# Block-sparse attention with a gated FFN: first loads split by head, row-tiled matmuls in all units, a new written order

## The chip, the cores and the metric

The kernel runs on one core of a Trainium2 chip. The metric is device time in microseconds (us) of one execution; lower is better. Three timed runs of the kernel before gave a median of 282.53 us (282.47 to 284.15).

## What is computed

```python
B, H, S, D = 4, 8, 768, 64
scores = q @ k.T / 8                       # per batch and head
mask   = window of +-1 block | first and last block row and column
         | 3 sampled blocks per block row  # blocks of 32
attn   = softmax(where(mask, scores, -1e9))
x      = (attn @ v), heads side by side    # 3072 tokens x 512
out    = (sigmoid(x @ w_gate) * (x @ w_val)) @ w_out   # 512 -> 1536 -> 512
```

Inputs and output are float32; the kernel computes in float16 with float32 sums.

## The kernel before, in words

**Units.** The work is cut into 12 units of 256 query tokens: 4 batches of 3 units. A unit has 4 pairs of heads. A pair has 3 steps (`Step`): each makes the scores of 256 keys by 256 queries for both heads (`qk`, line 546), ScalarE takes the exponential of the 128x1024 tile into a ring buffer `P` (`exp`, line 569), and VectorE multiplies it by the 0/1 mask (`mul`, line 574). In unit 0 the mask is added before the exponential instead, by extra matmuls of `bias` and the block-spread matrix `e64`, so its steps have twice the matmuls and no multiplication. After the three steps `pv` (line 595) multiplies P by `v` with a column of ones beside it (65 columns), `norm` divides by the sum on VectorE, and the pair's rows are turned into `xT`. Units 0 and 1 turn them by matmul (`turn`, line 623) with a copy out of PSUM (`evac`, on VectorE or ScalarE); later units use a DMA transpose (`xbar`, line 666).

**FFN.** Once all four pairs of a group of units are in `xT`, `Ffn.f` (line 735) makes the gate and value products, ScalarE takes tanh, VectorE multiplies them into `ht`, and `y` makes the output rows, which are copied out and stored. The first four groups are one unit each (matmuls of 256 columns), the last four are two units each (512 columns).

**Two ways to run a product of 128 rows.** `turns` (line 340) cuts each product into two of 64 rows, which run side by side in the two row halves of TensorE's array, on two PSUM banks; for that a job is run in two parts, and between them TensorE waits for the first part's last matmul (`nop`, line 345), so other work is put between. `whole` (line 357) issues one matmul over all 128 rows, in one part. Units below `WIDE = 2` use `whole` for PV and for the FFN's first products (`value`, line 634, and line 775); all the others use `turns`. Scores always have 64 rows. The last unit's output (`y_last`, line 889) is whole in both versions. The transposes of keys and queries that were loaded as 16 bit run in quarters of the array (64*64).

**Order.** Nothing reorders the instructions: a planner made the string `ORDER` (line 39) beforehand, which lists all tasks by number in the order in which every engine issues them, with the PSUM bank (`:2`, four banks m0 to m3), the engine where there are two (`A` ScalarE, `D` VectorE), and gates for loads (`@`). `j3` is a pair of matmuls of zeros (`idle`, line 313) into bank 3.

**Start.** SyncE's queue issues the constants, then the first two heads' keys as float32 (`k32`, lines 246 to 254); ScalarE's queue issues the sampled blocks, those heads' queries (`q32`), and one copy of the spread matrix; GpSimd's queue issues the other copy of it (line 256), for which it waits until VectorE has cleared `e64`, and then all that is in `FIRST` (line 36): keys, queries and values of the other heads, then the FFN's weights. The float32 heads are cast and paired (`pair`, line 473), turned by matmul (`turn`, line 477) and copied to `kT` and `qT`. `mask_blocks` (line 290) makes the block mask from the constants and the sampled blocks, and matmuls of it with `e64` (line 397) spread it to `bias` and `mb24`.

Of the kernel before, what the change touches and what calls it, by code (L numbers as in the profile page):

```python
# [12 lines left out]
f16 = mybir.dt.float16  # L13
# [22 lines left out]
FIRST = "k1 q1 v0 k2 q2 v1 k3 q3 v2 v3 r0 w0 r1 w1 r2 w2 r3 w3 w4 w5 o0 o1 o2"  # L36
FFN_LAG = 3
VW = 96
ORDER = """
j3 j3 j3 j3 0 j3 j3 j3 11D 1:0 8A 3:1 5D 12:2 6:3 4A 7D 2 13A 80:3 106:1 9:0 30:2 107A 10D 81D  # L40
15:1 31 34:0 16D j3 76:3 17:2 35 32:1 18D 77D 74:2 33 40:0 14 20:3 75D 41 44:1 21D 22:2 45 19 36:0
23D 25:3 27:2 37 26D 215@30 50:1 28D 46:3 51 82:2 48:0 83D 47 64:1 49 84:2 60:0 85D 65 38:3 29 61
56:2 39 66:1 57 42:0 67D 54:3 43D 52:1 165:0 53D 55 93:2 24 58:1 166 94 99:3 59 68:2 95:0 100 96D
181:1 69D 62:0 182 63D 78:3 102:2 162:0 79D 144@102 103 70:1 126:3 125@50 71D 183 163 164 111:1
127 119:2 131:0 120 128 167 112 104 138:3 122:2 132 145:1 123 133 121 139 124 169:0 146 140 147
72:2 170 86:3 159:1 73D 87 171 152:2 160 205:0 153 108:3 88 89:1 206 105@89 90 101 174:2 92@165
154 109 187@89 207 239:1 91 235@86 175 155:0 188:3 110 156 114@40 176 168@155 240 113 115:0 157
189 141:2 116 202:1 142 190 195:0 203 143 196 232:3 172:2 233 129:0 173 97:3 191:2 130 204 192A
193 98A 117:0 256 212:2 194 216 118A 213 184:3 177:0 217 178A 185 134:2 148:0 218 149D 135D 241
242:0 198:3 221A 252:2 214 199 136 179 219A 258 180 246:3 200 253 227 137 254 268:1 247 257 243  # L50
248 150 229:2 234 151 269 209:3 300:0 210 270 259 161 230 237 197 293:1 296:3 228 301 284:2 231
297 302 238 244 294 280:0 186 287:3 285 201@280 211 281 286 249:1 298 288 277:0 223:2 289 278 250
224 251 336:3 327:0 337 158@336 225 274 264:1 279 261:2 271:3 265 295 236 328 262 266 272 310:1
329 273 311 226 263 307:2 320:3 255 340 308 290 312 303:1 321 309 323:2 341 282 324 333:3 208 304
378@333 322 342 334 305 347:2 345A 343D 351:3 314:1 245@351 352 348 338 372:0 315 299@64 349 373
365:3 316 357@181 369 375:2 353 386:0 403@239 358:1 376 317 374 366 387 377 325 354:2 359 367 355
368 404:0 360 356 432:3 400:2 405 433 361 313@400 260 393:1 326@307 401 335 411:3 267@333 406 402
418:2 394 419 424@418 412 407 283@138 395 362:0 413 389:2 379:1 390 414 363 397:3 425:2 364 398
388 383 466:0 380 420 467 330 370 435:3 426 391 381 436 382 439:0 346 415 399 427 408:1 421:3 428
440 220 422 275 222 470:2 291 409 344 471 331 473:3 441 434 332 474 318 476:2 410 276 475 487:3  # L60
446:1 477 488 416 319 472 452 447 423 417 449:3 437 453 478 384 450 463:1 479 292 454 464 489
442:3 385 448 493:2 457A 451 455A 443 371 516:1 465 494 517 444 507:0 429 430 495 518 459:3 490:1
496 508 491 468 483:2 509 492 504:1 510 460 505 484 461 480:0 506 469 485 542:1 497:3 543 486 481
456 498 482 519:2 431 511:1 520 499 501:0 576:3 462 521 512 502 536:2 500 503 513 522:0 577 514
537 515 526:1 538 558:3 523 544 559 527 524 555:2 549:3 528 556 306 539 608:1 525 550 609 560 552
532:2 644:0 551 533 529:1 645 534 597:2 562 530 646 563 557 598 594:0 564 578 392@594 595 531
601:1 633@421 565D 567A 561@32 627:2 569:0 610 628 573:3 579@141 570 602 438@122 571 574 629
339@555 630:2 587:0 631 596 704@50 647:3 575 588 548@397 603 648 604 600@470 580:2 396 683@209 589
662:1 545:3 581 668@165 663 590 632 619:0 546 622:1 664 582 599 620 611:3 623 583 612 621 615:2
624 665:3 625 673:0 666 616 547 350 674 756:1 614@40 634:3 675 757 710 695 584:0 553 617 635 445  # L70
718@435 618 651:1 636 535@662 585 650@102 680:2 652 586 681 637 684:0 653 613 677:2 701:3 654 685
678 606 642 638:1 607 702 696 669:2 686 639 591 712:3 670 640 713 687 458 655:1 605 671 682 715:3
691:0 592 716 659 649 656 540 758 554 705:3 657 714 692 658 568 641 672 753:1 706 693 754 694 566
719:2 593 717 707 698:0 746:1 720 708 643 747 660 721 703 699 661 729:3 726:1 732 730 700 667
739:0 727 733 679 731 743:3 740 744 734 741 755 688:1 752 735A 722:0 728 689 737A 723 690 787:3
749:2 788 724 801:1 572 742 798:0 745 790:3 750 799 748 709 751 791 766:0 541 802 792 769:3 759
770 711 772:1 767 760 773 768 676 844:3 779:0 761 775:1 762A 764D 845 780 763 818:2 776 781 800
804:3 777 774 819 793:0 778 805 771 820 857:1 794 858 782:2 795 835:1 806 796 807 815:0 783 816
789 829:3 836 784 830 785 821:0 859 837 808:2 803 822 838 811:3 823 817 860:1 809 824 861 812 810
832:0 831 828 825:1 813 863:2 833 814 697 826 864 827 786 834 847:3 854:0 848 839:1 626 862 843  # L80
865 855 875:3 840 856 876 738 846 797 870:0 841 850:3 842 765 874 849 878:1 871 879 866 736 851
872 867:2 873 852 881:1 853 898:0 868 877 899 925:3 882 869 926 892:0 883 944:2 886:3 893 945 884
725 895:1 887 880 889:2 894 890 896 928:3 904 891 929 888 962:2 905 963 897 911:3 914 915:1 973:2
906 916 885 912 909A 921:1 913 974 946 922 924 927 923 907D 970:3 941:2 900 931 971 901:0 942 972
918:3 932 917 919 933 902 947:2 934D 954:3 936A 975 903 959:0 965:1 960 943 948 961 955 949 966
950 956 938:0 957 967 983:2 968 939 1004:3 976:1 940 1005 990:0 984 991 987:3 977 985 988 986
993:0 978 1016:2 980:3 1017 979 994 930 1011:1 995 981 996 1050:2 1012 982 1051 920 1007:0 1013
1052 1001:3 951:2 1014 1002 1008 992 952 1061:1 1022:3 953 1062 964 969 1042:2 1009 1003 1019:1
958 989 1023 1020 1010 1043 1024 1021 1053:1 1025 1044 1058:0 1045 997:3 1059 1054 998 1060 1055
1029:2 1035:0 999 1030 1056 1015 1026:3 1036 1018 1063 1027 1037 1047:2 1082:1 1006 1048 1031 1083  # L90
1028 1039:2 1038 1046 1071:3 1040 1032:0 1084 1041 908 1033 1049 1000 1072 1064:2 1034 1057 1073
1067:0 1065 1081 1068 1085 1069 937 1066 1070 1086 935 1074 910 1075 1087 1076 1090D 1100:3 1091
1079D 1096:0 1077D 1078 1101 1080 1097 1102 1132:2 1103 1098 1088A 1108:3 1099 1089 1120:1 1109
1112:0 1110 1121 1111 1113 1122 1092:3 1123 1114 1124:1 1115 1133 1093 1104:0 1094 1125 1095 1105
1126 1134 1136:3 1127 1106 1135 1116:1 1107 1128:2 1117 1137 1118 1129 1119 1138 1140:0 1139 1130
1141 1131 1142 1150:1 1151 1152 1143 1153 1144 1154 1145 1160:3 1146A 1148D 1161 1147 1162 1149
1155:2 1163 1156 1164 1157 1158 1159
"""
GAP, PV_HALF, F_HALF, Y_ONE = 0.3, 0.36, 0.875, 0.216
WIDE = 2  # L100
# [20 lines left out]
class Plan:  # L121
# [4 lines left out]

    def __init__(self, order, idle, hold):
        self.order, self.idle, self.hold = order.split(), idle, hold
        self.tasks, self.last = [], {}
# [5 lines left out]
    def run(self):  # L135
        done = set()
        for token in self.order:
            if token[0] == "j":
                self.idle(int(token[1:]))
                continue  # L140
            i, eng, slot, gate = re.fullmatch(r"(\d+)([PADGS]?)(?::(\d))?(?:@(\d+))?", token).groups()
            i = int(i)
            engines, fn, deps, more = self.tasks[i]
            assert i not in done and done.issuperset(deps)
            done.add(i)
            if slot is not None:
                more["take"].slot = int(slot)
            self.last[i] = fn(eng or engines[0][0])
            if gate is not None:
                self.hold(self.last[i], self.last[int(gate)])  # L150
# [4 lines left out]
def kernel(  # L155
# [46 lines left out]
    e64 = sing.tile([128, S], f16)  # L202
    nc.vector.memset(e64, 0.0)
# [42 lines left out]
    def first_heads(eng, dst, src, t0, t1):  # L246
        eng.dma_start(
            dst[:, :, t0:t1, :],
            src[0, 0:2].rearrange("h (p t) d -> p h t d", t=NT)[:, :, t0:t1, :],
        )  # L250

    nc.sync.dma_start(const, const_h.ap())
    nc.scalar.dma_start(sbi, sampled_blocks)
    first_heads(nc.sync, k32, k, 0, NT)
    first_heads(nc.scalar, q32, q, 0, 2)
    nc.gpsimd.dma_start(e64[0:NB], spread_h.ap())
# [28 lines left out]
    junk = sing.tile([128, 512], f16)  # L285
    nc.vector.memset(junk, 0.0)
# [3 lines left out]
    def mask_blocks(eng):  # L290
        sbf = sing.tile([NB, 3], f32, name="sbf")
# [811 lines left out]
```

## Time and profile before

| | |
|---|---|
| timed runs | 282.47, 282.53, 284.15 us |
| profiled execution | 281.96 us, of which the traced span is 280.2 us |
| mean granted TensorE clock | 0.994 |
| TensorE busy (PE) | 272.4 us, 97% of the span |
| ScalarE busy (ACT) | 192.1 us, 69% |
| VectorE busy (DVE) | 187.9 us, 67% |
| exponentials | 144 of 1.025 us |
| the last matmul ends | 276.97 us into the span |

PE's busy share counts overlapping, pipelined matmuls, so it is read beside the pitch: the time from one start to the next. Times in rows are microseconds from the start of the span; a bracket gives how long the engine was idle before the row and what released it. `64*128` in a matmul's row means that it used 64 rows of the array, `128*128` all of them, `64*64` a quarter.

### The profile page before, as it was taken

The numbers are of one execution on the slowest core, as the hardware profiler recorded it, in microseconds if no ns is written. First come the engines' busy times: TensorE is split into PE (matmuls) and PEld (weight loads), VectorE is DVE, ScalarE is ACT, GpSimd is POOL, SyncE is SP. The second block draws the span as 40 slices with busy tenths as digits, with TensorE's granted clock in tenths as the row PEclk, the third lists the DMA queues.
The fourth block names the chain that finished last, engine by engine and source line by source line (L and its number), as shares of the span: only waits on it lengthen the run. The fifth ranks groups of instructions, "written<-read, shape, count | busy, mean of one in ns | idle before, by whom it ended". The sixth has DMA issues, their size and how long they took to land.

```text
span 280.2 us, 10875 instructions
## 1 busy us (share of the span) xinstructions
PE 272.4 (97%) x4889; PEld 186.1 (66%) x4889; DVE 187.9 (67%) x387; ACT 192.1 (69%) x239; POOL 47.4 (17%) x70
## 2 busy tenths in 40 slices
PE   5999999999999999999999999999999999999995
PEld 2677786777899799766555655666656667555543
DVE  4667894788887888688778746875664888142421
ACT  3798888699897878898668866578677683023301
POOL 8975441011531000082400000000000000000000
PEclk9799999999999999999999999999999999999999
DMA  7999999765589975279967330041100012440003
GB/s 148 184 195 196 200 205 202 110 127 87 77 110 150 206 129 126 40 106 188 125 115 162 68 97 2 12 133 50 30 2 0 6 21 65 117 180 2 0 5 147
DMA packets 56679, 28.92 MB, mean 103 GB/s; under 512 B 33044, under 2 KB 53676, under 8 KB 56632
## 3 DMA queue, kind: packets, MB, share of 16 engines
q0 software_dynamic: 21552, 13.93, 35.6%
q1 hardware_dynamic: 34592, 13.99, 22.7%
q8 instruction: 38, 0.62, 0.9%
q10 hardware_dynamic: 488, 0.30, 0.4%
q14 instruction: 9, 0.07, 0.1%
HBM read 28.47 MB, written 6.29 MB: 124 GB/s over the span
## 4 chain that ended last, share of the span: by engine, by line
PE 91%; DMA 3%; ACT 2%; DVE 2%; issue 1%; SPq 0%; DVEq 0%
PE m L338 89%; DMA xT<-x 2%; DMA e<-bb_spread 1%; ACT P L570 1%; PE m L456 1%; DVE ysb L833 1%; ACT ysb L831 0%; PE m L451 0%; DVE kT L282 0%; DVE mask L282 0%; ACT mask L280 0%; SPq L667 0%; PE m L397 0%; DVE x L616 0%; PE m L315 0%
## 5 line engine op out<-in xcount | busy, mean ns | idle before, releaser
L570 ACT ACTIVATE P<-m 128x1024 f16<-128x1024 f32 x144 | 142.5, 1025 | 31.3 <-PE m L338 27.3
L338 PE MATMUL m<-xT,wv 64*128 64x512 f16 (+2 forms) x672 | 136.1, 331 | 0.3 <-issue 0.3
L338 PE MATMUL m<-xT,wg 64*128 64x512 f16 (+2 forms) x672 | 135.9, 331 | 0.1
L576 DVE TENSOR_TENSOR P<-P,mask 128x1024 f16<-128x1024 f16 x132 | 86.7, 686 | 11.1 <-ACT P L570 10.8
L338 PEld LDWEIGHTS <-wg 64*128 64x128 f16 (+1 forms) x672 | 61.8, 94 | 20.5 <-issue 2.0
L338 PEld LDWEIGHTS <-wv 64*128 64x128 f16 (+1 forms) x672 | 61.8, 94 | 15.9 <-issue 0.3
L338 PE MATMUL m<-wo,ht 64*128 64x512 f16 (+2 forms) x564 | 70.7, 372 | 0.0
L765 DVE SCALAR_TENSOR_TENSOR ht<-th,m 128x512 f16<-128x512 f32 x72 | 49.0, 686 | 30.6 <-ACT th L762 29.6
L762 ACT ACTIVATE th<-m 128x512 f32<-128x512 f32 x72 | 42.7, 598 | 36.0 <-PE m L338 35.3
L338 PE MATMUL m<-qT,kT 64*128 64x256 f16 x576 | 54.0, 272 | 0.3 <-DVE ysb L833 0.2
L338 PEld LDWEIGHTS <-P 64*128 64x128 f16 (+1 forms) x2112 | 46.2, 94 | 9.0 <-issue 1.1
L338 PE MATMUL m<-vex,P 64*128 64x65 f16 (+1 forms) x2112 | 48.2, 190 | 0.0
L338 PEld LDWEIGHTS <-ht 64*128 64x128 f16 (+1 forms) x564 | 30.5, 94 | 21.6 <-issue 1.3
L338 PEld LDWEIGHTS <-kT 64*128 64x128 f16 x576 | 27.4, 95 | 13.0 <-issue 1.7
L220 POOL DMA_DIRECT2D v<-in_v_dram x16 | 11.4, 717 | 65.3 <-PE m L338 56.5
L616 DVE TENSOR_TENSOR x<-m,rz 128x256 f16<-128x256 f32 x48 | 20.4, 425 | 1.7
L615 DVE RECIPROCAL rz<-m 128x4 f32<-128x4 f32 x48 | 8.7, 180 | 17.9 <-PE m L338 16.4
L220 POOL DMA_DIRECT2D q<-in_q_dram x19 | 13.6, 723 | 12.1 <-PE m L338 11.1
L831 ACT ACTIVATE ysb<-m 128x512 f32<-128x512 f32 x13 | 7.5, 597 | 10.6 <-PE m L338 9.9
L833 DVE TENSOR_SCALAR ysb<-m 128x512 f32<-128x512 f32 x9 | 6.1, 688 | 11.8 <-ACT ysb L831 5.5
L220 POOL DMA_DIRECT2D k<-in_k_dram x15 | 10.8, 723 | 6.1 <-PE m L338 5.5
L338 PE MATMUL m<-bias,e 64*128 64x256 f16 x48 | 6.9, 301 | 0.3
(46 smaller groups left out, 69.7 us busy)
## 6 DMA issues: line engine op xcount, KB each, us to landing
out_dram<-ysb SPq DMA_DIRECT2D x23, 256.0 KB, 2.4
v<-in_v_dram POOLq DMA_DIRECT2D x16, 192.0 KB, 5.5
k<-in_k_dram POOLq DMA_DIRECT2D x15, 192.0 KB, 5.9
q<-in_q_dram POOLq DMA_DIRECT2D x12, 192.0 KB, 7.1
wg<-in_moe_w_gate_dram POOLq DMA_DIRECT2D x6, 256.0 KB, 8.6
wv<-in_moe_w_val_dram POOLq DMA_DIRECT2D x6, 256.0 KB, 8.9
wo<-in_moe_w_out_dram POOLq DMA_DIRECT2D x3, 512.0 KB, 12.8
xT<-x SPq DMA_TRANSPOSE x40, 3.2
```

Source lines behind the costliest of these rows:

```text
L220: return nc.gpsimd.dma_start(dst[:, h0:h1, t0:t1, :], src[b, h0:h1].rearrange("h (p t) d -> p h t d", t=NT)[:, :, t0:t1, :],)
L338: return nc.tensor.matmul(out, lhsT, rhs, start=start, stop=stop, skip_group_check=True).ins
L456: nc.tensor.transpose(out16[a * D : (a + 1) * D, h, i * D : (i + 1) * D], tile_[rows, a], ident[rows, rows],)
L570: nc.scalar.activation(self.pt.rearrange("a h i n -> a (h i n)"), both(self.bank).rearrange("a h n -> a (h n)"), AF.Exp, bias=0.0, scale=SCALE
L576: nc.vector.tensor_tensor(self.pt, self.pt, m.unsqueeze(1).broadcast_to([128, 2, 2, UQ]), op=ALU.mult,)
L615: nc.vector.reciprocal(rz, self.acc[:, :, :, D : D + 1])
L616: nc.vector.tensor_tensor(self.x16.rearrange("a s h d -> a h s d"), self.acc[:, :, :, 0:D], rz.broadcast_to([128, 2, 2, D]), op=ALU.mult,)
L762: nc.scalar.activation(th, both(bank)[:, 0, :], AF.Tanh, bias=0.0, scale=0.5)
L765: nc.vector.scalar_tensor_tensor(self.ht[:, tiles[0] : tiles[-1] + 1, :], in0=th.rearrange("a (f n) -> a f n", n=self.w), scalar=1.0, in1= ...
L831: nc.scalar.activation(ysb, both(bank)[:, s, :], AF.Copy, bias=0.0, scale=0.5)
L833: nc.vector.tensor_scalar(ysb, in0=both(bank)[:, s, :], scalar1=0.5, scalar2=None, op0=ALU.mult)
```

## The change

`WIDE` goes from 2 to 0, so PV and the FFN of units 0 and 1 run in `turns` as well. The first two heads' keys and queries are loaded one head per queue, keys first, ahead of the constants and the sampled blocks. Both copies of the spread matrix come from the SyncE and ScalarE queues, so GpSimd's first load is that of the second pair's keys, and it waits for nothing. The tile of zeros is 128x128, is cleared first, and is broadcast; a new kind of zero matmul (`j2s`) has 128 columns in place of 512. There are 9 tokens of the long kind (8 before) and 5 short ones. The block mask is made with one cast and one reduction less. `ORDER` is a new string: every engine's order differs, the key transposes of the first heads now stand ahead of the mask matmuls, and the last unit's three output pieces come in another sequence. A split of the first FFN products into three chunks and one is written in as well, but with `EARLY = 0` no task uses it.

```diff
+EARLY = 0
...
-j3 j3 j3 j3 0 j3 j3 j3 11D 1:0 8A 3:1 5D 12:2 6:3 4A 7D 2 13A 80:3 106:1 9:0 30:2 107A 10D 81D
...
+j2 j2 j2 j2 j2 j2 8A 5D j2 0 9:0 11A j2s j2s 10D 1:1 12:2 3:3 2 13D j0s j1s j1s 4A 32:0 17:1 6:2
...
-WIDE = 2
+WIDE = 0
...
+    junk = sing.tile([128, 128], f16)
+    nc.vector.memset(junk, 0.0)
     nc.vector.memset(e64, 0.0)
...
-    def first_heads(eng, dst, src, t0, t1):
-        eng.dma_start(
-            dst[:, :, t0:t1, :],
-            src[0, 0:2].rearrange("h (p t) d -> p h t d", t=NT)[:, :, t0:t1, :],
-        )
-
+    def both_heads(dst, src, t0, t1):
+        for h, eng in ((0, nc.sync), (1, nc.scalar)):
+            eng.dma_start(
+                dst[:, h, t0:t1, :],
+                src[0, h].rearrange("(p t) d -> p t d", t=NT)[:, t0:t1, :],
+            )
+
+    both_heads(k32, k, 0, NT)
     nc.sync.dma_start(const, const_h.ap())
     nc.scalar.dma_start(sbi, sampled_blocks)
-    first_heads(nc.sync, k32, k, 0, NT)
-    first_heads(nc.scalar, q32, q, 0, 2)
-    nc.gpsimd.dma_start(e64[0:NB], spread_h.ap())
+    both_heads(q32, q, 0, 2)
+    nc.sync.dma_start(e64[0:NB], spread_h.ap())
     nc.scalar.dma_start(e64[D : D + NB], spread_h.ap())
...
-        sbf = sing.tile([NB, 3], f32, name="sbf")
-        nc.vector.tensor_copy(sbf, sbi.bitcast(u16)[:, 0:12:4])
...
-            sbf.unsqueeze(1).broadcast_to([NB, NB, 3]),
+            sbi.bitcast(u16)[:, 0:12:4].unsqueeze(1).broadcast_to([NB, NB, 3]),
...
-        for o in (0, D):
-            nc.vector.tensor_reduce(
-                mb16[0:NB, o : o + NB], mc, axis=mybir.AxisListType.X, op=ALU.max
-            )
+        nc.vector.tensor_reduce(
+            mb16[0:NB].rearrange("a (o n) -> a o n", n=D)[:, :, 0:NB],
+            mc.unsqueeze(1).broadcast_to([NB, 2, NB, 4]),
...
-    def idle(unit):
+    def idle(unit, kind):
+        n = 1 if kind == "s" else 4
         for i in range(2):
+            rows = slice(i * D, (i + 1) * D)
             nc.tensor.matmul(
-                units_ps[unit][:, i, :],
-                junk[i * D : (i + 1) * D, 0:128],
-                junk[i * D : (i + 1) * D, :],
+                units_ps[unit][:, i, 0 : n * 128].rearrange("a (x n) -> a x n", n=128),
+                junk[rows],
+                junk[rows].unsqueeze(1).broadcast_to([D, n, 128]),
```

## The prediction, made before the changed kernel ran

> **What bounds the kernel now.** I read the page first (busy digits, granted clock, chain), then the first 25 us engine by engine, then the pitch of matmuls.
>
> ```profile
> PE   5999999999999999999999999999999999999995
> ACT  3798888699897878898668866578677683023301
> PEclk9799999999999999999999999999999999999999
> PE 91%; DMA 3%; ACT 2%; DVE 2%; issue 1%; SPq 0%; DVEq 0%
> ```
>
> TensorE (PE) is the bound: 91% of the chain. Only three things can shorten the span: an earlier start, fewer holes between matmuls, or less matmul time. The clock is low in the second slice alone. The start, by the timeline:
>
> ```profile
> 0.74 0.35 SPq L252 DMA_DIRECT2D const<-bb_const  x1
> 1.15 0.50 SPq L247 DMA_DIRECT2D kp<-in_k_dram  x1
> 1.57 0.69 POOL L256 DMA_DIRECT2D e<-bb_spread  x1 [1.13 <-DVE e L203]
> ...
> 2.25 0.73 POOL L220 DMA_DIRECT2D k<-in_k_dram  x1
> ...
> 5.28 0.62 ACT L280 CAST qp<-kp 128x512 f16<-128x512 f32 x1 [3.26 <-DMA kp<-in_k_dram]
> 5.44 0.68 DVE L282 CAST qp<-kp 128x256 f16<-128x256 f32 x2 [1.78 <-DMA kp<-in_q_dram]
> 5.62 0.59 PE L397 MATMUL m<-e,mb 64*128 64x256 f16 x3 [0.79 <-DMA e<-bb_spread]
> ```
>
> Keys, queries and the spread matrix land within 0.35 us of each other, the spread last. ScalarE then carries the stage:
>
> ```profile
> 8.08 1.02 ACT L570 ACTIVATE P<-m 128x1024 f16<-128x1024 f32 x1
> 9.55 1.02 ACT L570 ACTIVATE P<-m 128x1024 f16<-128x1024 f32 x1 [0.45 <-PE m L338]
> 11.41 7.67 ACT L570 ACTIVATE P<-m 128x1024 f16<-128x1024 f32 x8 [0.84 <-DVE mask L282]
> 19.39 1.96 ACT L570 ACTIVATE P<-m 128x1024 f16<-128x1024 f32 x2 [0.31 <-PE m L338]
> ```
>
> Eight exponentials in 7.67 us are 0.96 us each, back to back. Unit 0's twelfth ends at 21.35. The FFN, which has matmuls in plenty, starts at 25.02; before that PE waits for exponentials, after it ScalarE waits for PE. The rows around that point show what a change of array mode costs:
>
> ```profile
> 24.77 0.32 PE L456 MATMUL m<-const,q 64*64 64x64 f16 x16 [0.15 <-ACT P L570]
> 25.02 0.28 PE L338 MATMUL m<-xT,wg 128*128 128x256 f16 x1
> ...
> 26.66 0.27 PE L338 MATMUL m<-xT,wv 128*128 128x256 f16 x1
> 26.87 0.61 PE L338 MATMUL m<-qT,kT 64*128 64x256 f16 x8
> 27.41 0.28 PE L338 MATMUL m<-xT,wg 128*128 128x256 f16 x1
> ```
>
> Whole matmuls start 0.109 us apart (16 from 25.02 to 26.66), but 26.66 to 26.87 is 0.21: 0.10 us lost. Back again, 8 score matmuls (four pairs of 0.107) need 0.43 of the 0.54 us: 0.11 lost. The same time is lost at each change of mode.
>
> **The change part by part.** The sum goes by the profiled execution: 281.96 us, 280.2 of it span. It is 0.57 below the median of 282.53, so I add the sum's difference to the median.
>
> 1. *No whole matmuls.* Their work costs the same either way: 16 whole FFN matmuls take 1.74 us, and 32 halves take 1.74 from 102.99 to 104.73; a pair's PV is 24 whole in 0.74 (33.98 to 34.82, less one change) and twice 0.37 as halves. What goes is the changes. Counting neighbours in the two programs gives 47 changes before and 23 after; from the FFN's start on, 25 and 5 (one group of query transposes and the last output). Those 20 at 0.095 to 0.10 save 1.9 us. The others lie in the stage that waits for ScalarE and are worth nothing; if that wait went, the remaining 4 would give 0.4. New is TensorE's wait between two half jobs. In the new order 0.2 us or more of other matmuls stand between the two in all early cases, so I take 0; the bound is 0.3 us in each of 20 jobs, half of it hidden: 3 us.
>
> 2. *First loads.* SyncE's queue now issues keys, constants, queries, spread; the keys go out at 0.74 in place of 1.15 (4.1 us to landing). By the issue alone they land at 4.9; with the constants (2.0 us) no longer ahead, perhaps 4.2: I take 4.5. The two casts (0.62) and eight transposes (0.3) end at 5.5, ahead of the mask rather than behind it. The spread, fourth in its queue, goes out at about 2.1; with 3.1 to 4.1 us to landing that is 5.2 to 6.2, and I take 5.8, late in the range, since 220 GB/s already move between 1.66 and 5.02 and GpSimd's keys now take part of that. From there: mask matmul 0.27, bias 0.41, copy of qT 0.29, scores 0.5, hand-overs 0.2: first exponential at 7.5 (7.0 to 8.0) against 8.08. The dropped cast (0.46) and reduction (0.2) on VectorE end by 3.7 in the old trace, ahead of the landings that are waited for: 0; were the landings 2 us earlier, they would count in full.
>
> 3. *GpSimd's loads* go out 1.5 us earlier (0.75 against 2.25), but the bytes ahead of the second pair are the same. By issue they land at 6.5, by bytes at 8.1, as the queries did; I take 7.8. In the new order the second scores are queued behind the second pair's transposes of queries (8) and keys (24): 7.8, then about 0.9 for the transposes, 0.84 for four score pairs at half clock (0.21 each in the old rows), 0.3 of latency: second exponential at 9.8, third at 10.9. Then ScalarE does a kT copy, which VectorE did (0.56 there; 0.80 by ScalarE's 768-wide cast): fourth exponential at 12.6 against 12.37. Nine at 0.96 end unit 0 at 21.3 against 21.35. What the start won has gone to that copy and to the bytes.
>
> 4. *What stands before the FFN on ScalarE.* In the new order the FFN's first matmul is behind a mask matmul whose bank is freed by a ScalarE copy to xT, and that copy is the second of two (0.38 each, 0.33 back to back) behind four exponentials of unit 1. 21.3 + 4 x 0.96 + 2 x 0.33 + 0.4 for hand-over and two short jobs gives 26.2, against 25.02. Bounds: 24.5 if the loads come by issue and the clock stays full; 27.5 with the latest loads and ScalarE holes like the old 0.31 + 0.2 + 0.2.
>
> 5. *From the FFN to the end.* Before, 276.97 - 25.02 = 251.95 us. Take off 1.9 (changes) and 0.2, since one more score job of unit 1 stands ahead of the FFN: 249.85. The old order has holes of 0.26 at 74 and 0.35 at 166 (two output copies in a row), 0.44 at 83 and 0.26 at 93 (DMA transposes), 0.17 at 122: 1.5 us. In the new order the output copies have more room, but two DMA transposes have only 4.4 and 4.7 us of matmuls between the PV that feeds them and the FFN that reads them (6.6 at the least before); norm (0.18 + 0.42) and the median 3.2 us to landing fit, the 5.5 us of the slowest rows would not. I take 0.2 gained, bounds 1.5 gained and 1.5 lost. Tail: ScalarE's 0.38 replaces VectorE's 0.42: 0.
>
> Sum: 26.2 + 249.65 = 275.85 against 276.97: 1.1 us less. Rounded with the tail to 1.2, that is 281.3 us.
>
> **The rivals.**
>
> *GpSimd's early loads hold up the first heads (slower).* The three queues feed the same stream, at its highest rate in just these microseconds (220 GB/s, then 154 and 185). If the spread lands at 6.6 and the second queries at 8.3, the first exponential is at 8.3, the fourth at 13.2, and the FFN starts at 26.8 + 0.7 for the old holes = 27.5, with no hole closed later: 277.4, and 283.0 us. It decides from an FFN start of 27.1 on. Against it: the keys' packets start first. The Trainium skill (DMA: Bandwidth & Descriptors, Queues, rings and completion order) says that each engine goes round-robin between queues by packets; by that rule this rival gains weight.
>
> *The start stays won.* If the clock stays full, the second and third scores come 0.5 us earlier each; with loads by issue the FFN starts at 24.8, and with 1 us of later holes closed PE ends at 273.7: 279.2 us. The row speaks against a full clock:
>
> ```profile
> 5.02:8.43 3.41, 2.00 (x55) 1.60 (x54) 2.09 (x6) 2.60 (x5) 3.35 (x6) 1.00 1.20 154
> 8.43:11.84 3.41, 3.41 (x51) 1.98 (x38) 2.11 (x6) 2.12 (x3) 3.14 (x5) 0.50 1.38 185
> ```
>
> PE was busy 2.00 of 3.41 us, and the next stretch had clock 0.50; the new order waits as much there, and 128-column zeros fill little. The Trainium skill (TensorE: Matmul & The Clock Gate, What's actually happening) wants a whole idle window of about 3.4 us before the clock halves; the longest idle before the drop is 0.79, so this trace disagrees. By that rule the new kernel, without such a gap, would stay at full clock, which is this rival.
>
> *DMA transposes come late* at both tight places, by 1 us each: 283.3 us.
>
> **How the numbers follow.** Forecast (ScalarE opens the FFN late, fewer changes repay it): 0.50, at 281.3, own range 280.3 to 282.3. Start won: 0.25. GpSimd slower: 0.17. Late transposes: 0.08. The range reaches from the start-won case, 279.2, to 283.4, beyond both slow cases. About 1% is what can be told from no change: under 279.7 is a little more than half of start-won and a little of the forecast, 0.17; over 285.4 needs both slow cases with half-job waits on top, 0.05; the rest is 0.78.
>
> **What would show it.** First exponential near 7.5, second near 9.8, first FFN matmul near 26.2, pitch of 0.107 per pair without 0.10 holes from 26 to 62, and a gap of 0 between half jobs. I am wrong if the FFN starts before 25 or after 27.1, or if holes of over 0.2 us stand behind 30.

## The result, and the profile after

Measured: 291.97 us median (289.65 to 292.2, five runs) against 282.53 for the kernel before; ratio 1.028, 95% interval 1.0215 to 1.0346. The change makes the kernel slower by 2.8%, where I forecast 0.4% faster. The profiled execution took 291.97 us, 290.2 of it span. I read the page first:

```profile
PE   5995999998998899999999999999999999999995
ACT  2697598857985787786896685378786863033300
PEclk9999799999999999999999999999999999999999
...
q8 instruction: 41, 0.67, 1.0%
...
PE 88%; ACT 3%; issue 3%; DMA 2%; DVE 1%; SPq 0%; ACTq 0%; DVEq 0%
```

TensorE has gaps in slices 4, 10, 13 and 14 (7.25 us each) that it did not have, and "issue" has 3% of the chain, 1% before: time in which TensorE waited for nothing that the profile shows. The page of before has this row for queue 8:

```profile
q8 instruction: 38, 0.62, 0.9%
```

The start of after, by the timeline (start, duration, engine, line; in brackets the idle time and what ended it):

```profile
1.24 0.83 POOL L225 DMA_DIRECT2D k<-in_k_dram  x1 [0.80 <-POOLq L1111]
...
4.04 0.62 ACT L286 CAST qp<-kp 128x512 f16<-128x512 f32 x1 [2.02 <-DMA kp<-in_k_dram]
...
7.57 0.40 ACT L286 CAST qp<-kp 128x256 f16<-128x256 f32 x1 [2.90 <-DMA kp<-in_q_dram]
7.78 0.37 PE L405 MATMUL m<-e,mb 64*128 64x256 f16 x1 [2.45 <-DMA e<-bb_spread]
...
10.17 1.02 ACT L578 ACTIVATE P<-m 128x1024 f16<-128x1024 f32 x1 [0.38 <-PE m L344]
12.07 2.01 ACT L578 ACTIVATE P<-m 128x1024 f16<-128x1024 f32 x2 [0.88 <-PE m L344]
```

The keys came 1.2 us earlier (5.28 before), but queries and spread matrix 2.1 and 2.2 us later, and the first exponential is at 10.17 against 8.08. TensorE's timeline up to the FFN:

```profile
21.97 0.33 PE L344 MATMUL m<-vex,P 64*128 64x65 f16 x10
23.42 0.75 PE L344 MATMUL m<-vex,P 64*128 64x65 f16 x38 [1.12 <-issue]
...
27.21 0.30 PE L344 MATMUL m<-vex,P 64*128 64x65 f16 x8
29.62 0.45 PE L344 MATMUL m<-vex,P 64*128 64x65 f16 x16 [2.11 <-issue]
...
31.81 0.41 PE L344 MATMUL m<-xT,wg 64*128 64x256 f16 x1
```

Two PV half jobs are torn apart. All their operands had been there since before their first matmul, no semaphore stands between the parts, and yet TensorE stood still for 1.12 and 2.11 us. The FFN starts at 31.81 (25.02 before). After the second hole the clock is low for one stretch (columns: stretch, its length, busy time of PE, PEld, DVE, ACT, POOL, granted clock, DMA share, GB/s):

```profile
26.47:29.88 3.41, 0.75 (x33) 0.50 (x30) 1.18 (x3) 1.55 (x2) 2.06 (x4) 1.00 1.45 197
29.88:33.29 3.41, 3.41 (x63) 2.85 (x57) 2.79 (x7) 2.68 (x4) 0.23 (x1) 0.50 1.42 204
```

More holes of this kind follow at 67, 86, 90 and 97 us. TensorE's program ends at 286.66 (276.97).

**Where the holes are.** I counted TensorE's instructions (a weight load, a matmul and each of its few semaphore rows count as one) up to every hole. The seven that are to be explained (at 22, 27, 41, 67, 86, 90 and 97 us) all lie behind number 192 of a run of 256, counting from 0. Queue 8 moves packets of 16,384 bytes; 41 of them (38 before) at 256 instructions each make 10,496 (9,728), nearly all of TensorE's 10,570 weight loads and matmuls (9,778). So TensorE gets its program in blocks of 256. The profile puts the holes at 86 and 90 down to a tanh of ScalarE; it had ended 0.5 and 0.3 us before TensorE went on, so the one at 90 may in part be that wait. Put side by side from the trace's records, in us (a block "starts" with its first instruction; the wait is from the start of the block before to the start of the packet; the hole is TensorE's idle time):

```
kernel, block   block before   packet   wait  landed   first instruction  hole
                starts         starts                  of the new block
after, 2        17.57          21.17    3.60  22.15    23.42              1.1
after, 3        23.42          27.25    3.83  28.21    29.62              2.1
after, 10       63.96          66.00    2.04  67.07    68.36              1.0
after, 15       91.58          96.41    4.83  97.35    98.87              1.4
before, 2       16.21          19.45    3.24  20.40    21.89              none
before, 11      78.19          81.34    3.15  82.36    83.83              0.3
before, 30     199.16         199.08   -0.08 200.27   209.48              none
```

So a block is fetched while the one before it runs. In these two kernels the wait goes from -1.9 us, late in the program, to 4.8 us while loads run; the packet mostly takes 0.9 to 1.4 us, and the new block's first instruction follows at the earliest 1.22 us after the landing. While DMA is busy, a block must therefore last about 3.8 + 0.95 + 1.3 = 6.1 us, by this estimate, if TensorE is not to wait. By the durations in the prediction, whole FFN matmuls use 256 instructions in 14 us, FFN halves in 7, whole PV matmuls in 3.9 and PV halves in 2.0. The change doubled the instructions of units 0 and 1's PV and first FFN products. The kernel before stood at the edge: its hole at 83, which I had put down to a transpose, stands at the start of block 11.

### The profile page after: what moved, and what is told of

It reads as the page before. It is cut to its first block, busy times and chain, and to the rows that moved or that the text cites. A ratio compares the mean times of both kernels' runs of the same rounds, so it can differ in the third digit from the quotient of the medians.

```text
span 290.2 us, 11672 instructions
## 1 busy us (share of the span) xinstructions
PE 273.7 (94%) x5285; PEld 190.3 (66%) x5285; DVE 188.6 (65%) x388; ACT 189.2 (65%) x236; POOL 47.4 (16%) x69
## 4 chain that ended last, share of the span: by engine, by line
PE 88%; ACT 3%; issue 3%; DMA 2%; DVE 1%; SPq 0%; ACTq 0%; DVEq 0%
PE m L344 86%; ACT P L578 3%; DMA e<-bb_spread 2%; PE m L464 1%; DVE mask L288 0%; PE m L459 0%; ACT th L770 0%; PE m L405 0%; SPq L253 0%; DVE ysb L857 0%; PE m L321 0%; ACT ysb L855 0%; DVE x L624 0%; DVE qT L288 0%; SPq L259 0%
## 5 line engine op out<-in xcount | busy, mean ns | idle before, releaser
L344 PE MATMUL m<-xT,wv 64*128 64x256 f16 (+1 forms) x768 | 138.6, 324 | 1.1 <-issue 1.0
L344 PE MATMUL m<-xT,wg 64*128 64x256 f16 (+1 forms) x768 | 138.1, 324 | 1.1 <-ACT th L770 0.8
L344 PEld LDWEIGHTS <-wg 64*128 64x128 f16 x768 | 70.8, 94 | 19.4 <-issue 0.3
L344 PEld LDWEIGHTS <-wv 64*128 64x128 f16 x768 | 70.6, 94 | 18.4 <-issue 2.8
L344 PE MATMUL m<-qT,kT 64*128 64x256 f16 x576 | 55.0, 274 | 0.1
L344 PEld LDWEIGHTS <-P 64*128 64x128 f16 x2304 | 45.6, 94 | 12.7 <-issue 5.9
L344 PE MATMUL m<-vex,P 64*128 64x65 f16 x2304 | 47.6, 190 | 5.4 <-issue 4.6
L344 PEld LDWEIGHTS <-kT 64*128 64x128 f16 x576 | 30.2, 95 | 12.0 <-issue 0.5
L623 DVE RECIPROCAL rz<-m 128x4 f32<-128x4 f32 x48 | 8.6, 178 | 23.4 <-PE m L344 22.9
L855 ACT ACTIVATE ysb<-m 128x512 f32<-128x512 f32 x11 | 6.4, 602 | 13.0 <-PE m L344 11.8
L857 DVE TENSOR_SCALAR ysb<-m 128x512 f32<-128x512 f32 x11 | 7.3, 686 | 9.5 <-PE m L344 8.3
```

The lines of the kernel that those rows point to most:

```text
L344: return nc.tensor.matmul(out, lhsT, rhs, start=start, stop=stop, skip_group_check=True).ins
L623: nc.vector.reciprocal(rz, self.acc[:, :, :, D : D + 1])
L855: nc.scalar.activation(ysb, both(bank)[:, s, :], AF.Copy, bias=0.0, scale=0.5)
L857: nc.vector.tensor_scalar(ysb, in0=both(bank)[:, s, :], scalar1=0.5, scalar2=None, op0=ALU.mult)
```

## The experiments

Theory A: the holes are instruction blocks that arrive late, because half jobs use them up faster than they can be fetched beside the loads. Theory B: the late first loads cause the loss. Theory C: the new order does, by its own waits.

**1. Whole jobs in the new order** (after_whole):

```diff
-            if first is None:
-                whole(mms, self.bank)
+            if self.n < 2:
+                if first:
+                    whole(mms, self.bank)
```

and the same for the FFN.

> The changed kernel with one edit: in units 0 and 1 each PV job and FFN job is whole again (issued in the place of its first half; the second half issues nothing). First loads and order stay as changed. Theory A (instruction blocks): TensorE's instructions come in blocks of 256 over the DMA engines that also carry the loads, and half jobs use up a block in half the time, so TensorE stands at the end of a block until the next has come; the seven holes of 0.8 to 2.3 us at block ends (8.8 us in all) shrink to under 2 us, the mode changes come back (about 1.9 us), the late start stays (first exponential near 10.2): 284 to 287 us. Theory B (late first loads cause the loss, the holes follow from it): holes and start stay, mode changes are added: 292 to 294. Theory C (the new order is at fault): 291 to 294.

Measured: ratio 1.0523 (1.0468 to 1.0578), 297.99 us. All three missed. The holes at 22 and 27 us are gone, but others stand at other block ends, in jobs that this edit doesn't touch:

```profile
66.58 0.47 PE L344 MATMUL m<-vex,P 64*128 64x65 f16 x20
68.94 0.23 PE L344 MATMUL m<-vex,P 64*128 64x65 f16 x4 [1.89 <-issue]
```

Four of 2.0, 1.5, 0.7 and 1.0 us over the pitch stand between 66 and 102, all behind number 192 of a run of 256. The edit takes out 768 instructions, which is three blocks exactly, so behind unit 1's FFN the blocks end in the same places as in after. One PV job, first in after, then in this run, where the hole is the longer (the second rows go on behind the end of the view):

```profile
85.29 0.53 PE L344 MATMUL m<-vex,P 64*128 64x65 f16 x24
86.48 0.70 PE L344 MATMUL m<-vex,P 64*128 64x65 f16 x35 [0.65 <-ACT th L770]
```

```profile
88.87 0.53 PE L344 MATMUL m<-vex,P 64*128 64x65 f16 x24
90.79 0.40 PE L344 MATMUL m<-vex,P 64*128 64x65 f16 x15 [1.39 <-ACT P L578]
```

The exponential that the last row names had ended 0.35 us before, so a part of that hole may be its doing. The holes of after at 99 and 185 us come back in the same matmuls too, at 102 (0.8 us, put down to "issue") and 189. Mode changes went from 23 to 57, 34 times 0.1 us. And whole jobs in an order made for halves wait for exponentials, for example 0.48 at 41. So theory A holds for where TensorE stands still, but the holes behind 80 us are not made by the halves of units 0 and 1, as my sum had it: they stand in jobs that are halves in both kernels, and the new order alone, with whole jobs in units 0 and 1, has them too.

**2. Half jobs in the old order** (before_halves):

```diff
             if first is None:
-                whole(mms, self.bank)
+                turns(mms, self.bank, True)
+                turns(mms, self.bank, False)
```

and the same for the FFN.

> The kernel before with one edit: each whole PV and FFN job of units 0 and 1 is done as its two halves, one behind the other in the same place. First loads and order stay as before. Theory A (instruction blocks): new holes of 0.5 to 2 us at block ends between 15 and 40 us and between 60 and 100 us, less about 1.9 us of mode changes: 284 to 289 us. Theories B and C: no new holes, mode changes gone: 280 to 281.5, as my prediction's first step had it.

Measured: 1.0319 (1.0264 to 1.0373), 292.01 us, over A's range. TensorE's timeline and its waits (waited for, us in total, times, longest):

```profile
22.36 0.28 PE L338 MATMUL m<-bias,e 64*128 64x256 f16 x2 [1.62 <-issue]
28.56 0.29 PE L451 MATMUL m<-const,x 64*128 64x64 f16 x4 [3.12 <-issue]
```

```profile
PEld L338 <- PE m L338: 5.8, 20, 0.5
```

Three holes at block ends (1.6, 3.1, and 0.8 at 54), none of over 0.3 behind them, and half clock from 27.7 to 34.5. What I had not expected is the second view: with nothing between the two halves each of the 20 jobs waits for its own first half, 0.22 us longer than the usual pitch, 4.4 us in all. This run therefore overstates half jobs by up to 4.4 us. The new order has no such wait.

**3. Old first loads under the new order** (after_old_loads): `both_heads` and the order of the first issues are replaced by the lines of before.

> The changed kernel with the first loads of before (constants first, both heads of the keys on one queue and of the queries on the other, the upper spread matrix on GpSimd's queue ahead of its loads); order and half jobs stay as changed. Theory A (instruction blocks): the first exponential comes back to 8.0 to 8.4 us, but the holes at block ends stay, 5 us or more of them: 287 to 290.5 us. Theory B (late first loads): start and holes both go: 280 to 283. Theory C (the order): 288 to 291 without holes at block ends.

Measured: 1.0243 (1.0198 to 1.0289), 290.17 us. The holes at 22, 27 and 67 stay (22.9: 1.3; 29.1: 2.3; 67.9: 1.0, from start to start). Of those at 41, 86, 90 and 97 only 0.3 us at 85 is left, and new ones of 1.2 and 0.8 stand at 103 and 107, one and two blocks behind the last of them. The first exponential is at 8.91 (A had 8.0 to 8.4). B falls: the first loads are at most a few tenths of a per cent, and the intervals of the two ratios overlap.

**4. Loads for nothing in the kernel before** (before_more_loads):

```diff
+            load = nc.gpsimd.dma_start(
+                extra[i % 3],
+                k[i % B, 0:1].rearrange("h (p t) d -> p h t d", t=NT),
+            )
```

twelve times at each of three places.

> The kernel before with three bursts of twelve loads each that nothing reads (one head of keys, 196 KB each, into spare tiles), issued by GpSimd behind the 69th, 99th and 140th score job (near 104, 150 and 226 us in the kernel before); TensorE's program is the same. Theory A (instruction blocks): the blocks fetched under a burst arrive 3 to 4 us after the last block end rather than 0.5, and holes of 1 to 2.5 us appear at one to five block ends within the bursts and nowhere else: 285 to 290 us. If the holes come from half jobs or from the order in another way than by the fetch: 282 to 283.5.

Measured: 1.0127 (1.0059 to 1.0195), 287.54 us. The profile is that of the longest of the four runs (290.97 us; the others took 284.95 to 288.29), so it shows what the bursts can do, and not what the median is made of. The waits of the packets under the bursts went from 0.3 (block 16) to 3.0, from -0.1 (block 23) to 2.3, from 0.8 (block 25) to 2.8 and from 0.8 (block 35) to 2.4 us, with TensorE's program unchanged. Only one such block was short enough to run out:

```profile
112.92 0.39 PE L352 MATMUL m<-qT,kT 64*128 64x256 f16 x4 [2.23 <-DMA kT<-kp]
...
163.48 0.45 PE L352 MATMUL m<-vex,P 64*128 64x65 f16 x18 [1.47 <-issue]
```

The other large holes, as at 112.92, are keys whose DMA transposes came late beside the bursts. So loads do delay the fetch; the time of this run is only in part its price.

**5. The block ends moved** (after_shift): the first five zero matmul pairs are cut up, which puts 128 more instructions ahead of everything else.

> The changed kernel with the first five zero matmul pairs cut into narrower ones of about the same columns: 128 more TensorE instructions ahead of everything else, all else as changed. Theory A (instruction blocks of 256): the holes put down to issue, which stood at instruction 192 of each block of 256 as I count them in the changed kernel's trace, move to other matmuls, those 128 instructions earlier in the program: near 20, 25, 65, 87 and 98 us rather than 22, 27, 67, 86 and 97, with sums of 6 to 11 us; time 288 to 295. If the holes belong to the order or to the half jobs (the bank's semaphore): they stay at the same matmuls, 290 to 292.5.

Measured: 1.0399 (1.0338 to 1.0461), 294.88 us. The holes stand at 19.8, 26.0, 65.8, 88.9 and 100.4 us, again behind number 192 of a run of 256, and now in other matmuls:

```profile
19.84 0.22 PE L478 MATMUL m<-const,q 64*64 64x64 f16 x2 [1.58 <-issue]
26.04 1.34 PE L358 MATMUL m<-vex,P 64*128 64x65 f16 x42 [1.54 <-issue]
```

Nothing of order, banks or jobs changed, so neither C nor the bank's semaphore can make a hole move in this way.

**6. Batches 2 and 3 not loaded** (after_quiet): their loads are left out of the plan's run, and the output of these batches is wrong.

> The changed kernel without the loads of batches 2 and 3: their attention is computed from batch 1's keys, queries and values that are still in SBUF, so that part of the output is left wrong; TensorE's, ScalarE's and VectorE's programs are the same. Theory A (instruction blocks): the fetches between 79 and 105 us start within 1 us of the block's end before, and the holes at 86, 90 and 97 us (0.5, 0.8, 1.4 us) go; those at 22 and 27 us, which stand under batch 0's loads, stay, and perhaps that at 67: 287 to 290 us. If the holes have nothing to do with transfers: 290.5 to 292.5, all holes there.

Measured: 1.0201 (1.0156 to 1.0245), 288.85 us. As A said: the packets of blocks 13 to 15 wait 1.1, 0.6 and 0 us (2.8, 2.6 and 4.8 in after), and the holes at 86, 90 and 97 are gone. The same PV jobs, first in after, then in this run:

```profile
96.84 0.65 PE L344 MATMUL m<-vex,P 64*128 64x65 f16 x32
98.87 0.81 PE L344 MATMUL m<-vex,P 64*128 64x65 f16 x42 [1.37 <-issue]
```

```profile
95.63 1.62 PE L345 MATMUL m<-vex,P 64*128 64x65 f16 x96
```

The holes at 23.4, 29.6 and 68.9 stay.

**7. GpSimd's loads as late as before** (after_pool_late):

```diff
+    late = sing.tile([128, 1024], f16)
+    nc.gpsimd.memset(late, 0.0)
```

> The changed kernel with one more instruction: GpSimd fills an unused tile of 128x1024 ahead of its first load, so that its loads go out about 1 us later, as they did before. If GpSimd's early packets are what held up the first heads: queries and spread matrix land by 5.5 to 6.0 us in place of 7.3 to 7.5, the first exponential is at 7.5 to 9, and the time 289 to 290.5. If the spread and queries are late because they stand behind keys and constants on their own queues: they land after 6.5 us as before this edit, 291 to 292.5.

Measured: 1.0242 (1.0189 to 1.0294), 290.51 us. Queries are cast at 6.26 and the spread matrix is used at 6.66, between the two cases. With the changed loads the spread was used at 7.78 in the profile of after, but at 6.7 to 7.3 in experiments 1, 5, 6, 11 and 13. GpSimd's early packets cost some tenths of a us; most of the delay against 5.62 is there without them.

**8. New first loads under the old order** (before_both_heads), the spread matrix still on GpSimd's queue.

> The kernel before with only the new loads of the first heads (keys one head per queue and ahead of the constants, then the queries one head per queue); the upper spread matrix stays on GpSimd's queue ahead of its loads, and order and whole jobs stay as before. If the early keys are worth something by themselves: casts at 4.1 to 4.6 us, first exponential 7.3 to 8.0 us, 281 to 282.3. If the queries or the spread matrix, now last on their queues, come later than before: first exponential 8.2 to 9.5, 283 to 284. By the theory of instruction blocks nothing changes behind 30 us.

Measured: 1.0008 (0.9978 to 1.0037), 283.46 us. Keys are cast at 3.88, queries at 6.58, the spread is used at 5.86, the first exponential is at 9.78: the second case, with no measurable effect on the time.

**9 and 10. Weights filled with zeros in place of loading, and batches 2 and 3 not loaded** (after_quieter, before_quieter).

> The changed kernel without the loads of batches 2 and 3 and without the loads of the three weight matrices, which GpSimd fills with zeros instead: the output is wrong, the programs of the other engines are the same. Theory A (instruction blocks): with the weights' packets gone the fetches between 12 and 35 us start within 1.5 us of the block's end before, the holes at 22 and 27 us (1.3 and 2.2 us) go too, and with them the half clock behind 30 us; the FFN starts by 29.0 rather than 31.7: 283 to 286.5 us. If those two holes belong to the order or the half jobs: 287.5 to 290 us, as without batches 2 and 3 alone.

> Control to the run above: the kernel before without the same loads (output wrong in the same way). Theory A: it has hardly a hole at a block's end, so it gains 0.5 to 1.5 us: 281 to 282.5. If missing transfers speed up any kernel (memory ports, landings of other loads), it gains as much as the changed kernel does: 276 to 279.

Measured: 1.0607 (1.0559 to 1.0656) and 1.046 (1.0369 to 1.0551), 299.76 and 298.45 us. Neither tells the theories apart, since the fills bring a delay of their own. In after_quieter, by VectorE's timeline:

```profile
12.06 15.78 DVE L533 COPY vex<-v 128x768 f16<-128x768 f16 x1
```

This copy takes 0.35 us in after_quiet. It lasted as long as GpSimd's fills went on, and kept masks and first PV jobs waiting.

**11. Only PV whole** (after_pv_whole): the first half of the diff of experiment 1.

> The changed kernel with the eight PV jobs of units 0 and 1 whole again (in the place of the first half), the FFN jobs still in halves. Theory A (instruction blocks): PV halves use 48 instructions in 0.37 us, FFN halves 64 in 1.75 us, so it is the PV halves that empty a block too fast; the holes at 22 and 27 us go, the FFN starts by 29 us; 16 more mode changes cost at most 1.6; behind 60 us the blocks end 384 instructions earlier or later in other jobs, so holes there move: 287 to 291 us. If FFN halves matter as much: holes of 1 us or more between 25 and 60 us remain, 291 to 294.

Measured: 1.0341 (1.0272 to 1.0411), 293.51 us. The holes at 22 and 27 are gone and the FFN starts at 28.28, so PV halves made them; but at the blocks' new ends one of 2.12 us stands at 86 and one of 1.6 at 63.7, and the time is over A's range. This edit takes out 384 instructions, one and a half blocks; experiment 5 put in 128, half a block. Both move the blocks' ends by half a block, and the holes at 63.7, 86.5 and 98.5 here stand in the same matmuls as those at 65.8, 88.9 and 100.4 there: two edits with nothing else in common, and of the three theories only A explains it.

**12. Keys of the first heads in two parts** (before_split_keys).

> The kernel before with the keys of the first two heads loaded in two parts: the two token tiles that the first scores need at the place of the old load, the other four behind the spread matrix on SyncE's queue. If the first exponential waits for bytes: queries and spread matrix land 0.5 to 1 us earlier, the first exponential is 0.5 to 1 us earlier than with the old loads in the same clock (7.3 to 9.0), 281.5 to 282.8 us. If what the start wins is lost again to ScalarE's later waits or to the clock's low window: 282.8 to 283.6, same.

Measured: 0.9997 (0.9967 to 1.0026), 282.6 us. First exponential at 8.06, spread used at 5.60 (8.08 and 5.62 before). Fewer bytes ahead brought the queries earlier (cast at 4.71, 5.44 before), but not the spread or the first exponential.

**13 and 14. Few weights loaded, batches 2 and 3 not loaded, nothing filled** (after_few_weights, before_few_weights).

```diff
-(wg, wv)[g][rows, c, f * 128 : (f + 1) * 128]
+(wg, wv)[g][rows, c, f % 2 * 128 : (f % 2 + 1) * 128]
```

> The changed kernel without the loads of batches 2 and 3, and with only the first sixth of the gate and value weights and the first third of the output weights loaded; every FFN job reads those (output wrong; the programs of TensorE, ScalarE, VectorE and SyncE are the same, GpSimd only issues fewer loads and fills nothing). Theory A (instruction blocks): the fetches between 17 and 35 us start within 1.5 us of the block's end before, the holes at 22 and 27 us go, the FFN starts by 29.5 us and not 31.7, and from there on it is 250 to 251.5 us: 282.5 to 286 us. If those holes belong to the order or the half jobs: 287.5 to 290, as without batches 2 and 3 alone.

> Control: the kernel before without the same loads (output wrong in the same way). Theory A: it gains only what its few holes at block ends cost, 0.5 to 1.5 us: 281 to 282.5 us. If missing transfers speed up any kernel: it gains as much as the changed kernel, 275 to 279 us.

Measured: 1.0081 (1.0045 to 1.0118), 285.09 us, and 0.9958 (0.9925 to 0.9992), 282.1 us. TensorE's timeline of after_few_weights:

```profile
20.96 0.33 PE L345 MATMUL m<-vex,P 64*128 64x65 f16 x10
22.36 0.76 PE L345 MATMUL m<-vex,P 64*128 64x65 f16 x38 [1.06 <-issue]
...
26.14 0.54 PE L345 MATMUL m<-vex,P 64*128 64x65 f16 x24
...
28.10 0.27 PE L345 MATMUL m<-xT,wg 64*128 64x256 f16 x1
```

The job that was torn for 2.11 us runs through (its block's packet waited 1.15 us in place of 3.83), no stretch of low clock follows it, and the FFN starts at 28.10. The hole at 21 stays: its packet still waited 3.30 us, at a time when batch 0's own loads, which this kernel keeps, were running. Without these loads the changed kernel sheds 2.0 of its 2.8%, and the kernel before gets 0.4% faster. So 1.6 of the 2.8% hang on these loads; the other 1.2% stay without them.

No version that does the whole work was measurably faster than the kernel before.

## Why the prediction was wrong

**Step 1, no whole matmuls: here it failed.** "Their work costs the same either way" is true of the array: with the holes taken out, the FFN part is as forecast. It is not true of the instruction stream. I compared durations and never counted instructions, though the page had the fetch queue as a row and "issue" as a part of the chain. Half jobs put 768 more instructions (the zero matmuls 24) into blocks that must each last 6 us while loads run. The holes at 22, 27, 41 and 68, some 4.6 us, stand in jobs that the change cut in halves (though at the last of these block ends TensorE stands still with whole jobs too, 68.9 us in experiment 1). The other 3.4 us of holes (86, 91, 99 and 185) do not come from the halves: 768 instructions are three blocks, so behind unit 1's FFN the new order and the 24 settle in which jobs a block ends, and the prediction had no term for that either. Which of these two it is was not tested. What else the step said held: 23 changes, 5 of them behind the FFN's start, and no wait between half jobs in the new order. That wait exists and is 0.22 us where nothing stands between (experiment 2), within my bound of 0.3.

**Step 2, first loads: the landings were mis-sized.** Keys 4.04 (forecast 4.5). Queries and spread came at 7.57 and 7.78, outside 5.2 to 6.2; the first exponential at 10.17 (forecast 7.5), and at 8.4 to 9.5 in six other kernels with the same loads. I took the spread from its issue and the old issue-to-landing times. Part of the scatter is the clock: with the old loads and the old order it is at 8.08 in the profile of before and at 9.29 in before_halves, where the spread came as early (5.68) but the clock, by the matmuls' pitch of 0.21 us a pair, stayed at half until 10.6; so 1.2 us of scatter is not the change's. In the time the first loads are worth less than the measurement can tell: 1.028 against 1.0243 and 1.0242 (experiments 3 and 7), and 1.0008 in the old order.

**Step 3** inherits this: second exponential 12.07 (9.8), unit 0's twelfth ends at 23.3 (21.3). GpSimd's loads went out at 1.24 (forecast 0.75, 2.25 before), and the second pair still did not land earlier: 8.15 and 8.36 us, against 7.69 and 8.08 before.

**Step 4, from the twelfth exponential to the FFN: right but for the holes.** Forecast 26.2 - 21.3 = 4.9 us. After: 31.8 - 23.3 = 8.5. Of this, 2.1 are the hole at 27, and 0.8 is idle time of ScalarE between the next exponentials (0.19 and 0.62), which I put down to the hole at 22; the last 1.9 us ran at half clock. In after_few_weights, without the second hole, it is 28.1 - 22.3 = 5.8, less 0.8 of the same idle time: 5.0.

**Step 5, from the FFN on: the holes were mis-sized.** Forecast 249.65, with 0.2 gained on holes and at the worst 1.5 lost; measured 254.84. Six holes at block ends (41, 68, 86, 91, 99 and 185 us), each less the usual 0.1 of pitch, are 4.8 us, and 1.48 us at half clock lose 0.7. What is left is 249.3, which agrees with the forecast 1.9 us for the dropped mode changes. Both signs of being wrong that I had named came: an FFN start after 27.1 and holes of over 0.2 us behind 30.

**The rivals.** GpSimd's early loads (283.0 us, an FFN start after 27.1): the FFN did start later, but mostly for another reason; experiments 3 and 7 leave this at a few tenths of a per cent. "The start stays won" fell with the first exponential. Late transposes: one hole of 0.84 us, at 209 us in after_few_weights, and one of 0.68 at 215 in after_old_loads, none of that size put down to them in after. The case that came true, a slower kernel by the instruction fetch, was not among them.

TensorE's end came 9.7 us later in the profiles. The FFN's start is 6.8 of that: 2.0 for the later twelfth exponential, 1.2 that step 4 had forecast, 2.9 for the two holes, and 0.7 left over, which the half clock may account for. Behind the FFN's start 2.9 are left: 4.8 of holes and 0.7 of low clock, less 1.9 of mode changes and 0.4 for the hole at 83 before, give 3.2. What stays open is why the packet waits: the records show when it starts, not what stands ahead of it. Whether a rearranged load plan would free the changed kernel of its holes was not tried.

## What to carry to other kernels

Count an edit's instructions as well as its durations: where an engine runs through 256 small instructions faster than a block can be fetched beside the running loads (about 6 us here by estimate; with little DMA a block of 2.7 us, the one ahead of the hole at 185, was still too short), it stands still, and the profile mostly says "issue", in the middle of a job. Such holes sit at a fixed count of instructions, so an edit ahead of them moves them, unless it adds or takes whole blocks of 256; look at which jobs the blocks end in before judging an edit by its time. Half jobs that save mode changes pay only where the stream has room for twice the instructions.

## What the runs showed of the hardware

- The Trainium skill (Runtime: NRT & Kernel Launch, Instruction fetch mechanics) says that instructions come in blocks of 16 KiB, 256 at a time, over the engine's own DMA queue: the trace agrees, in 41 packets of 16,384 bytes. It also holds the fetch to be hidden, since issue is slower than the fill: here 256 instructions ran in 3.9 us (23.42 to 27.32) and the next block's first one came 6.2 us after 23.42, so this trace disagrees.
- The clock halved after a stretch with TensorE busy 0.75 of 3.41 us and a longest gap of 2.11 us (after), as it did in the prediction's row with 2.00 busy: neither was idle throughout.
- A VectorE copy of 0.35 us took 15.78 while GpSimd filled memory (experiment 9). The Trainium skill (SBUF — State Buffer, Terms) says that the two share a port pair which one holds exclusively while the other is blocked; the run agrees, and there the copy got no turn between the fills.
